# Top-k attention with a tanh-shrink layer: the first matrix of the last two units as seven products of quarters

## The chip, the core and the metric

The kernel runs on one core of one Trainium2 chip. A core has five engines with queues of their own that meet through semaphores: TensorE (PE, matrix products; PEld are its weight loads), VectorE (DVE), ScalarE (ACT), GpSimd (POOL) and SyncE (SP, which issues most transfers). The metric is the device time of one execution in microseconds, as a median over runs; less is better. The profile comes from one execution of its own, with a time of its own; its span is the stretch between the first and the last instruction that the profiler saw.

## The reference

```
scores = 1/sqrt(D) * q @ k^T                 # B=8, H=8, S=576, D=64, fp32
kth    = the 32nd largest of each row
attn   = softmax of the scores >= kth, 0 elsewhere, sum + 1e-9
x      = attn @ v, heads side by side: 4608 tokens x 512
h      = x @ w_in                            # 512 x 2048
g      = h - tanh(h)
out    = g @ w_out                           # 2048 x 512
```

All of it is fp32. The change concerns `h = x @ w_in` and `g` for the last 512 of the 4608 tokens.

## The kernel before

**Steps.** `plan` lists the attention as steps: a step is 128 queries of a pair of heads (`hp`, 4 pairs) of one batch element. A step goes through `scores` (PE), `search` (DVE, the 32nd largest of each row), `threshold` (POOL), `mask` (ACT L436, then POOL L439 and L443: z and the flags `bad`), `expo` (ACT L459), the reciprocal (DVE, `invert`, L478), `divide` (ACT L485), `turn_z` (DVE transposition of blocks, L517), `spread_keys` (SP: out to DRAM and back, L522 and L534) and five steps later `values` (PE L582, then the copy ACT L602 into the activations `xT` or `xTr`). The function `between(i)` puts the reciprocal, `divide` and `turn_z` of the step before last into the search of the current step; after the last step (n == NS) no search is left, and they follow each other.

**Units.** When the four pairs of heads of a token block are there, it becomes a unit of the feed-forward part: 17 units of 256 tokens (tag xT; xTr for the remainders, 64 rows of each of four batch elements) and two of 128. The last two of all are the unit of the remainders of b 4 to 7 (here "rest", complete in the first half of b 7) and the unit of the query tiles 2 and 3 of b 7 ("last"). A unit of 256 is 30 items of work:

- 16 items of `ffn_h`: 8 matmuls each (two column halves by `by_columns`, w_in stationary, 256 tokens moving), and after every second item tanh and copy on ACT out of a PSUM bank (L652, L653) and a subtract on POOL (L654) into `g`, which has two buffers of 128x2048.
- 14 items of `ffn_p`: the second matrix as seven products of quarters (the `ORDER` of Strassen and Winograd), each in two halves k, in two PSUM banks hx and hy that take turns. The sums of quarters of g (`sum_up`, L727) and the joins of the result (L774) are done by POOL, the copies out of PSUM by ACT (L786 to L803). The sums of w_out's quarters were made once, earlier, by POOL (`combine`), and lie in `more` and in DRAM.

**Order.** The order on each engine is the order in which the program issues (`manual_schedule`). Per step, `rate` works out how many items are to be dealt, from the work at hand and the units that come, and `deal` puts them between the parts of the step. What is left after the last step is issued at the end, `for x in work`. Buffers that come from a pool (`thpool` 4, `gpool` 2, `kqpool`, `scpool`, `tpool`, `ldpool`) wait for the last reader of the buffer that they take over.

**The end.** After the last step: a reduction of all flags `bad` on DVE (L1086), a product of one column, and a branch to an exact second run, which isn't taken with these inputs.

Of the kernel before, what the change touches and what calls it, by code (L numbers as in the profile page):

```python
# [8 lines left out]
AF = mybir.ActivationFunctionType  # L9
ALU = mybir.AluOpType  # L10
FP32 = mybir.dt.float32
# [8 lines left out]
J = 4  # L20
# [20 lines left out]
class Unit:  # L41
# [3 lines left out]
    def __init__(self, blocks, tag):  # L45
        self.blocks, self.tag = blocks, tag
        self.n = 128 * len(blocks)
        self.combines = False
        self.items = 16 if self.n == 128 else 30
        self.xT = None  # L50
        self.g = []
# [3 lines left out]
def kernel(  # L55
# [9 lines left out]
    nc = tc.nc  # L65
    P = nc.NUM_PARTITIONS
    B, H, S, D = q.shape
# [44 lines left out]
    def h_bank(k, name):  # L112
        return h_ps.tile([P, 512], FP32, tag=f"h{k}", name=name)

    def next_h(name):
        bank[0] ^= 1
        return h_bank(bank[0], name)
# [243 lines left out]
    def search(n, exact, between):  # L361

        x = st[n]
        sc, ps = x["sc"], x.pop("ps")
        m = x["m"] = mpool.tile([P, 2, TOP], FP32, tag="m", name="m")
        rounds = TOP // 8  # L370
        if exact:
            whole = ab[:, 0 : 2 * S].rearrange("p (t k) -> p t k", t=2)
            seen = [[sc[:, t].rearrange("p s k -> p (s k)") for t in range(2)]]
            seen += [[whole[:, t] for t in range(2)]] * (rounds - 1)
            left = seen[1:]
        else:
            top = x["top"] = tpool.tile([P, 2, S4 + Q], FP32, tag="top", name="top")
            near, far = ps[:, :, 0, 0:S2], sc[:, :, 1, :]
            a, b = half_max, ps[:, :, 0, S2 : S2 + S4]
            nc.vector.tensor_tensor(b, near[:, :, S4:], far[:, :, S4:], ALU.max)  # L380
            nc.vector.tensor_tensor(a, near[:, :, 0:S4], far[:, :, 0:S4], ALU.max)  # L381

            def thirds(y):
                return y.rearrange("p t (r k) -> p t r k", r=NL)

            nc.vector.tensor_tensor(low[:, :, :, 0:W2], thirds(near), thirds(far), ALU.min)  # L386
            nc.vector.tensor_tensor(low[:, :, ::-1, W2:], thirds(a), thirds(b), ALU.min)
            nc.vector.tensor_tensor(top[:, :, 0:S4], a, b, ALU.max)  # L388
            for t in range(2):
                for i in range(NL):  # L390
                    o = S4 + 8 * i
                    nc.vector.max(top[:, t, o : o + 8], low[:, t, i, :])  # L392
            seen = [[top[:, t, 0:S4] for t in range(2)], [top[:, t] for t in range(2)]]
            seen += [[rest[:, t] for t in range(2)]] * (rounds - 2)
            left = [seen[0], *seen[2:]]
        between(-1)
        for i in range(rounds):
            m8 = slice(8 * i, 8 * i + 8)
            for t in range(2):
                nc.vector.max(m[:, t, m8], seen[i][t])  # L400
            if i < rounds - 1:
                for t in range(2):
                    nc.vector.match_replace(left[i][t], m[:, t, m8], seen[i][t], NEG)  # L403
            between(i)
# [210 lines left out]
    def xt(u):  # L615
        if u.xT is None:
            p = xpool if u.tag == "xT" else xrpool
            u.xT = p.tile([P, CD, N], FP32, tag=u.tag, name=u.tag)
        return u.xT
# [3 lines left out]
    def by_columns(acc, lhs, rhs, start, stop):  # L623

        for t in range(2):
            nc.tensor.matmul(  # L626
                acc[half(t)], lhs[:, half(t)], rhs, start=start, stop=stop, skip_group_check=True
            )
# [83 lines left out]
    def quarters(u, k):  # L712

        x = u.g[k][:].rearrange("p m (f t n) -> p m f t n", f=2, t=2)
        return [[x[:, :, f, t, :] for f in range(2)] for t in range(2)]

    def sum_up(u, k, x, ms=slice(0, 4)):

        (a11, a12), (a21, a22) = quarters(u, k)
        s1 = sums[k]  # L720
        out_, a, b, op = {
            "S1": (s1, a21, a22, ALU.add),
            "S3": (a21, a21, a11, ALU.subtract),
            "S2": (a11, s1, a11, ALU.subtract),
            "S4": (a12, a12, a11, ALU.subtract),
        }[x]
        nc.gpsimd.tensor_tensor(out_[:, ms], a[:, ms], b[:, ms], op)  # L727

    ORDER = [("A11", "B11"), ("A12", "B21"), ("S2", "T2"), ("S3", "T3"), ("S1", "T1"), ("A22", "T4"), ("S4", "B22")]
    def bring(x):  # L730
# [103 lines left out]
    def ffn(u):  # L834

        nh = CF * u.n // (2 * P)
        full = len(u.blocks) == 2
        for item in range(nh):
            f = (item + 1) * CF // nh - 1
            yield CD * (f // FJ + 1), u, lambda item=item: (ffn_full if full else ffn_h)(u, item)  # L840
        if not full:
            for part in range(CF // 2):
                yield CD * (WJ + part // 2 + 1), None, lambda part=part: ffn_small_o(u, part)
            return
        for item in range(2 * len(ORDER)):
            yield 2 * WJ * CD, None, lambda item=item: ffn_p(u, item)
# [5 lines left out]
    def plan():  # L852
        steps.clear(), done.clear()

        def block(b, qt):
            return [(slice(0, P), out[b * S + qt * P : b * S + (qt + 1) * P, :])]

        rest = None
        for b in range(B):
            if b % 4 == 0:  # L860
                rest = Unit(
                    [
                        [(half(i), out[(b + k + i) * S + JP : (b + k + i + 1) * S, :]) for i in range(2)]
                        for k in (0, 2)
                    ],
                    "xTr",
                )

            parts = [(0, 1), (2, 3)]
            if b == 0:  # L870
                parts[0:1] = [(0,), (1,)]
            for a, qts in enumerate(parts):
                unit = Unit([block(b, qt) for qt in qts], "xT")
                pe = b == 0
                unit.combines = pe and a == 1
                for hp in range(NHP):
                    for i, qt in enumerate(qts):
                        steps.append(Step(b, hp, qt, unit, 0, i, len(qts), pe, a))
                    if hp == NHP - 1:
                        done[len(steps) - 1] = unit  # L880
                    if hp % 2 and a == (0 if b == B - 1 else len(parts) - 1):
                        steps.append(Step(b, hp - 1, J, rest, b % 4 * R, pe=pe, part=a))
                        if hp == NHP - 1 and b % 4 == 3:
                            done[len(steps) - 1] = rest
        for g, after in zip(steps, steps[1:]):
            if after.pe and not after.rem and not g.pe:
                g.lag = 3
# [4 lines left out]
    def run(exact):  # L892
# [80 lines left out]
        def here(i):  # L973
            return 0 <= n + i < NS
# [55 lines left out]
        for n in range(-4, NS + LAG):  # L1030
            pe = here(-2) and steps[n - 2].pe
            def due():
                for m in (n - LAG, n - LAG + 1, n - LAG + 2):
                    if 0 <= m < NS and steps[m].last and steps[m].lag == n - m:
                        values(m)

            if n < NEAR:
                due()
            share, usable, now[0] = rate(), converted[0], n
            if pe:  # L1040
                w = turn_pe(n - 2)
                next(w)
            if here(-1):
                mask(n - 1, exact)
            if here(0):
                search(n, exact, between)
            elif here(-2):
                for i in (-1, 0, LATE):
                    between(i)
            if pe:  # L1050
                spread(n - 2)
            deal(0.0 if pe else 0.4)
            if n >= NEAR:
                due()
            for x in coming_back:
                next(x, None)
            coming_back.clear()
            if here(1):
                scores(n + 1)
            if pe:  # L1060
                next(w)
            if here(0):
                threshold(n, exact)
            if here(-1):
                expo(n - 1)
            deal(0.8 if pe else 0.2)
            if pe and steps[n - 2].last:
                values(n - 2)
            deal(0.0 if pe else 0.2)
            if here(-2) and not pe and steps[n - 2].last:  # L1070
                coming_back.append(spread_keys(n - 2))
                next(coming_back[0])
            for fn in todo.pop(n, []):
                fn()
            deal(0.2)
# [48 lines left out]
```

## Time and profile before

| what | us |
|---|---|
| median of 3 runs (1480.71, 1480.95, 1483.43) | 1480.95 |
| profiled execution, its own time | 1481.03 |
| its span | 1479.2 |
| PE busy | 1371.2 (93%) |
| DVE busy | 1281.5 (87%) |
| POOL busy | 1113.0 (75%) |
| ACT busy | 1030.9 (70%) |
| mean granted clock of PE | 0.974 |

Shares over the whole span mix two stages. Up to about 1310 us every step's search runs on DVE; after that DVE's share falls to nothing in the slices of the profile and PE's is 9 tenths or more. The changed units lie in that last stage. An instruction's record gives its start and duration; on PE, neighbouring records overlap, so the start-to-start distance is what a matmul costs. A fp32 matmul of this kernel leaves two records.

### The profile page before, as it was taken

The page shows a single profiled execution, that of the slowest core. Times are in us where ns is not written, and L with a number is a line of the kernel's source. Part 1 is how long each engine was busy: PE and PEld are TensorE (multiplying, and loading weights), DVE is VectorE, ACT ScalarE, POOL GpSimd, SP SyncE. Part 2 cuts the span into 40 slices and gives each one's busy share as a digit, 9 for nine tenths or more (in the row PEclk, how much of TensorE's full clock was granted, in tenths as well). Part 3 has the DMA queues.
Part 4 walks back from the last instruction along what each step waited for, and adds up shares of the span by engine and source line. Part 5 has one row for each costly group of instructions (what it writes and reads, how often), then busy time and mean ns, then how long its engine had stood idle before and what let it go on. Part 6 is the DMA issues. An engine that isn't in the chain of part 4 may idle for free.

```text
span 1479.2 us, 35177 instructions
## 1 busy us (share of the span) xinstructions
PE 1371.2 (93%) x12036; PEld 876.7 (59%) x12036; DVE 1281.5 (87%) x4906; ACT 1030.9 (70%) x1922; POOL 1113.0 (75%) x1607
## 2 busy tenths in 40 slices
PE   4667898889999898999999999999999999999998
PEld 2455565556666565656666666666665666656665
DVE  7999887999999999999999999999999999873000
ACT  4776677768787777777777777777777777664221
POOL 3887689968788786969696969696878797766523
PEclk9788999999999999999999999999999999999999
DMA  9955102776776676676766766667666666633311
GB/s 263 360 219 184 28 21 70 192 197 161 193 182 187 162 195 178 170 194 161 179 182 185 170 181 168 175 162 203 172 180 180 166 165 189 174 106 118 101 30 46
DMA packets 241084, 242.25 MB, mean 164 GB/s; under 512 B 177408, under 2 KB 185600, under 8 KB 233728
## 3 DMA queue, kind: packets, MB, share of 16 engines
q1 hardware_dynamic: 239120, 239.69, 60.0%
q8 instruction: 98, 1.61, 0.5%
q14 instruction: 90, 0.74, 0.2%
q10 hardware_dynamic: 1776, 0.22, 0.1%
HBM read 153.99 MB, written 85.85 MB: 162 GB/s over the span
## 4 chain that ended last, share of the span: by engine, by line
PE 44%; DVE 35%; POOL 9%; DMA 5%; ACT 4%; issue 2%; SPq 1%; DVEq 0%; ACTq 0%; POOLq 0%
PE hps L626 17%; PE hx L626 8%; PE hy L626 6%; DVE m L400 6%; PE scps L350 5%; PE av L582 5%; DVE top L392 5%; DVE zx L517 4%; DVE rest L403 4%; DVE ab L386 3%; POOL z L439 3%; DVE top L403 2%; DVE ab L381 2%; POOL g L654 2%; DVE scps L380 2%
## 5 line engine op out<-in xcount | busy, mean ns | idle before, releaser
L439 POOL TENSOR_TENSOR z<-sc,z 128x576 f32<-128x576 f32 x288 | 407.5, 1437 | 66.7 <-ACT z L436 66.3
L626 PE MATMUL hps<-xT,w_in 128*64 128x256 f32 x3840 | 435.8, 382 | 3.5 <-ACT g L653 3.5
L626 PEld LDWEIGHTS hps<-xT,w_in 128*64 128x64 f32 x3840 | 270.0, 137 | 160.0 <-issue 24.0
L654 POOL TENSOR_TENSOR g<-g,th 128x512 f32<-128x512 f32 x144 | 184.5, 1282 | 93.6 <-ACT g L653 91.8
L485 ACT ACTIVATE z<-z,rd 128x576 f32<-128x576 f32 x252 | 181.1, 767 | 83.9 <-DVE rd L478 82.1
L459 ACT ACTIVATE z<-z,nb 128x576 f32<-128x576 f32 x288 | 222.0, 777 | 13.0 <-POOL z L439 12.9
L436 ACT ACTIVATE z<-sc,tb 128x576 f32<-128x576 f32 x288 | 208.4, 776 | 25.1 <-POOL tb L417 20.0
L358 ACT COPY sc<-scps 128x1152 f32<-128x1152 f32 x144 | 161.1, 1118 | 49.9 <-PE scps L350 49.4
L392 DVE MAX8 top<-ab 128x8 f32<-128x144 f32 x864 | 194.7, 295 | 0.0
L517 DVE STREAM_TRANSPOSE zx<-z 128x1152 f32<-128x1152 f32 x126 | 171.6, 1362 | 23.7 <-ACT z L485 18.0
L350 PE MATMUL scps<-kT,qT 64*128 64x288 f32 (+1 forms) x1120 | 160.8, 438 | 30.1 <-DVE top L388 29.0
L400 DVE MAX8 m<-rest 128x8 f32<-128x168 f32 x576 | 161.6, 322 | 0.0
L400 DVE MAX8 m<-top 128x8 f32<-128x144 f32 (+1 forms) x576 | 152.8, 307 | 0.0
L350 PEld LDWEIGHTS scps<-kT,qT 64*128 64x128 f32 (+1 forms) x1120 | 87.8, 180 | 88.8 <-ACT z L436 26.4
L652 ACT ACTIVATE th<-hps 128x512 f32<-128x512 f32 x144 | 84.7, 588 | 71.9 <-PE hps L626 65.7
L626 PE MATMUL hx<-w_out,g 128*64 128x256 f32 x1088 | 129.6, 385 | 2.5 <-POOL g L654 2.5
L626 PE MATMUL hy<-more,g 128*64 128x256 f32 x1088 | 125.4, 380 | 0.0
L417 POOL TENSOR_SCALAR tb<-m 128x1 f32<-128x1 f32 x288 | 84.6, 303 | 31.7 <-DVE m L400 31.3
L386 DVE TENSOR_TENSOR ab<-scps,sc 128x576 f32<-128x576 f32 x144 | 107.7, 748 | 0.0
L626 PEld LDWEIGHTS hx<-w_out,g 128*64 128x64 f32 x1088 | 76.4, 138 | 49.5 <-POOL g L654 5.8
L626 PEld LDWEIGHTS hy<-more,g 128*64 128x64 f32 x1088 | 76.7, 137 | 42.9 <-issue 6.0
L443 POOL TENSOR_SCALAR bad<-top,tb 128x3 uint8<-128x3 f32 x288 | 97.1, 344 | 0.1
(126 smaller groups left out, 2349.6 us busy)
## 6 DMA issues: line engine op xcount, KB each, us to landing
there<-zx SPq DMA_DIRECT2D x56, 1152.0 KB, 4.8
spare<-there SPq DMA_DIRECT2D x224, 288.0 KB, 5.5
more<-kept_T SPq DMA_DIRECT2D x34, 512.0 KB, 3.8
out_dram<-ot SPq DMA_DIRECT2D x32, 256.0 KB, 2.9
there<-zx SPq DMA_DIRECT2D x14, 576.0 KB, 6.8
spare<-there SPq DMA_DIRECT2D x56, 144.0 KB, 3.1
vb<-in_v_dram SPq DMA_DIRECT2D x48, 128.0 KB, 5.4
kin<-in_k_dram SPq DMA_DIRECT2D x84, 72.0 KB, 4.4
```

What stands on the lines that cost most here:

```text
L350: nc.tensor.matmul(ps[rows, t, s, 0:S2], qT[g.b, g.hp + i, g.part][half(t), qs], kT[g.b, g.hp + i][half(t), ks], start=True, stop=True,)
L358: nc.scalar.copy(sc[:], ps[:, :, :, 0:S2])
L386: nc.vector.tensor_tensor(low[:, :, :, 0:W2], thirds(near), thirds(far), ALU.min)
L392: nc.vector.max(top[:, t, o : o + 8], low[:, t, i, :])
L400: nc.vector.max(m[:, t, m8], seen[i][t])
L436: nc.scalar.activation(zv[:, t, :], scf[:, t, :], AF.Relu, bias=tb[:, t : t + 1], scale=-BIG)
L439: nc.gpsimd.tensor_tensor(zv[:, t, :], scf[:, t, :], zv[:, t, :], ALU.subtract)
L459: nc.scalar.activation(x["zv"][:, t, :], x["zv"][:, t, :], AF.Exp, bias=x["nb"][:, t : t + 1], scale=scale, accum_out=den[:, t : t + 1],)
L485: nc.scalar.activation(x, x, AF.Copy, scale=rds[n][:, g.i, t : t + 1])
L517: nc.vector.transpose(tiles(zx, g.nq)[:, :, :, g.i, :].rearrange("p c k j -> p k c j"), z[:].rearrange("p (k c j) -> p k c j", c=NG, j=G),)
L626: nc.tensor.matmul(acc[half(t)], lhs[:, half(t)], rhs, start=start, stop=stop, skip_group_check=True)
L654: nc.gpsimd.tensor_tensor(g, g, th[:], ALU.subtract)
```

## The change

`Unit.tail` marks the last two units. For them the first matrix is done by 14 items of `ffn_s` in place of 16 of `ffn_h`, so such a unit has 28 items. `ffn_s` runs the same seven products as `ffn_p`, twice (k = 0, 1: the first and the second 1024 columns of w_in), each of 16 matmuls with 64 stationary columns and 128 moving tokens. The quarters are halves of the 512 rows and of the columns for w_in, halves of the rows and of the 256 tokens for x.

- `sides(k)` forms S1 to S4 of w_in[2k] and w_in[2k+1]: 8 instructions of 128x512 on DVE. `sides(0)` stands after the reciprocal and `divide` of step NS−2, `sides(1)` after its `turn_z`. The 16 results go to places that the attention no longer uses (`places`: ab, et_rem, one buffer of kin, four of kT, one of vb, three of sc).
- `tokens(u)` forms T1 to T4 of the unit's activations: 4 instructions of 128x256 on DVE, at the unit's first item.
- A product is copied out of PSUM by ACT; `join` adds on DVE, tanh on ACT, the subtract on POOL.
- `sum_up` of a tail unit (sums of quarters of g for the second matrix) runs on DVE; on POOL in all other units.

In the order of the instructions: on PE the scores of the last step and the values of head pair 1 of the last batch stand earlier against the first-matrix work around them; on ACT the masks of the last two steps (L436) stand one copy earlier. SP's order is the same.

```diff
@@ -46,6 +46,7 @@
         self.blocks, self.tag = blocks, tag
         self.n = 128 * len(blocks)
         self.combines = False
+        self.tail = False
         self.items = 16 if self.n == 128 else 30
         self.xT = None
         self.g = []
@@ -714,6 +715,106 @@
         x = u.g[k][:].rearrange("p m (f t n) -> p m f t n", f=2, t=2)
         return [[x[:, :, f, t, :] for f in range(2)] for t in range(2)]
 
+    left, right_of = {}, {}
+
+    def places():
+
+        yield from (ab[:, 0:512], ab[:, 512:1024], et_rem[:, 0:512], et_rem[:, 512:1024])
+        yield ldpool.tile([P, S], FP32, tag="kin", name="kin")[:, 0:512]
+        for x in range(NHP):
+            yield kqpool.tile([P, S], FP32, tag="kT", name="kT")[:, 0:512]
+        y = kqpool.tile([P, 2, J, D], FP32, tag="vb", name="vb", bufs=3)[:]
+        yield y.rearrange("p t c d -> p (t c d)")
+        for x in range(3):
+            y = scpool.tile([P, 2, 2, S2], FP32, tag="sc", name="sc")[:].rearrange("p t s k -> p (t s k)")
+            yield from (y[:, 0:512], y[:, 512:1024])
+
+    def sides(k):
+
+        for j in (2 * k, 2 * k + 1):
+            w = w_in[j][:].rearrange("p (q c) (m r n) -> p q c m r n", q=2, m=2, r=2)
+            (a11, a12), (a21, a22) = [[w[:, q, :, :, r, :] for q in range(2)] for r in range(2)]
+            new = []
+            for x in range(4):
+                new.append(next(space[0]).rearrange("p (c m n) -> p c m n", c=2, m=2))
+            s1, s2, s3, s4 = new
+            nc.vector.tensor_tensor(s1, a21, a22, ALU.add)
+            nc.vector.tensor_tensor(s2, s1, a11, ALU.subtract)
+            nc.vector.tensor_tensor(s3, a11, a21, ALU.subtract)
+            nc.vector.tensor_tensor(s4, a12, s2, ALU.subtract)
+            left[j] = {"A11": a11, "A12": a12, "A22": a22, "S1": s1, "S2": s2, "S3": s3, "S4": s4}
+
+    space = [None]
+
+    def tokens(u):
+
+        x = xt(u)[:].rearrange("p (q c) (t n) -> p q c t n", q=2, t=2)
+        (b11, b12), (b21, b22) = [[x[:, q, :, t, :] for t in range(2)] for q in range(2)]
+        ys = [rest[:].rearrange("p t k -> p (t k)")]
+        for i in range(2):
+            ys.append(tpool.tile([P, 2, S4 + Q], FP32, tag="top", name="top")[:].rearrange("p t k -> p (t k)"))
+        ys.append(ldpool.tile([P, S - 2 * P], FP32, tag="qin", name="qin")[:])
+        t1, t2, t3, t4 = [y[:, 0 : 2 * P].rearrange("p (c n) -> p c n", c=2) for y in ys]
+        nc.vector.tensor_tensor(t1, b12, b11, ALU.subtract)
+        nc.vector.tensor_tensor(t2, b22, t1, ALU.subtract)
+        nc.vector.tensor_tensor(t3, b22, b12, ALU.subtract)
+        nc.vector.tensor_tensor(t4, b21, t2, ALU.subtract)
+        right_of[u] = {"B11": b11, "B21": b21, "B22": b22, "T1": t1, "T2": t2, "T3": t3, "T4": t4}
+
+    def ffn_s(u, item):
+
+        k, i = item // len(ORDER), item % len(ORDER)
+        if item == 0:
+            tokens(u)
+        if i == 0:
+            cur[u] = [next_h("hx"), None]
+            u.g.append(gpool.tile([P, 4, 512], FP32, tag="g", name="g"))
+        if i == 1:
+            cur[u][1] = h_bank(bank[0] ^ 1, "hy")
+        acc = cur[u][i % 2][:].rearrange("p (m n) -> p m n", n=P)
+        a, b = ORDER[i]
+        for m in range(4):
+            lhs = left[2 * k + m // 2][a][:, :, m % 2, :]
+            for c in range(2):
+                by_columns(acc[:, m, :], lhs[:, c, :], right_of[u][b][:, c, :], i in (0, 1, 3) and m + c == 0, m == 3 and c == 1)
+        (g11, g21), (g12, g22) = quarters(u, k)
+
+        def own(x):
+            return thpool.tile([P, 512], FP32, tag="th", name=x)[:].rearrange("p (m n) -> p m n", n=P)
+
+        def join(x, y):
+            nc.vector.tensor_tensor(x, x, y, ALU.add)
+
+        def shrink(x, y):
+            th = own("th")
+            nc.scalar.activation(th, y, AF.Tanh)
+            if y is not x:
+                nc.scalar.copy(x, y)
+            nc.gpsimd.tensor_tensor(x, x, th, ALU.subtract)
+
+        if i in (0, 3, 5):
+            y = own("hp")
+            nc.scalar.copy(y, acc)
+            if i == 5:
+                join(g21, y)
+                shrink(g21, g21)
+            else:
+                u.part = y
+        elif i == 1:
+            nc.scalar.copy(g11, acc)
+            join(g11, u.part)
+            shrink(g11, g11)
+        elif i == 2:
+            nc.scalar.copy(g21, acc)
+        elif i == 4:
+            nc.scalar.copy(g22, acc)
+            join(g22, u.part)
+            shrink(g22, g22)
+        else:
+            shrink(g12, acc)
+            for x in ("S1", "S3"):
+                sum_up(u, k, x, slice(0, 2) if k else slice(0, 4))
+
     def sum_up(u, k, x, ms=slice(0, 4)):
 
         (a11, a12), (a21, a22) = quarters(u, k)
@@ -724,7 +825,8 @@
             "S2": (a11, s1, a11, ALU.subtract),
             "S4": (a12, a12, a11, ALU.subtract),
         }[x]
-        nc.gpsimd.tensor_tensor(out_[:, ms], a[:, ms], b[:, ms], op)
+        engine = nc.vector if u.tail else nc.gpsimd
+        engine.tensor_tensor(out_[:, ms], a[:, ms], b[:, ms], op)
 
     ORDER = [("A11", "B11"), ("A12", "B21"), ("S2", "T2"), ("S3", "T3"), ("S1", "T1"), ("A22", "T4"), ("S4", "B22")]
     def bring(x):
@@ -835,6 +937,10 @@
 
         nh = CF * u.n // (2 * P)
         full = len(u.blocks) == 2
+        if u.tail:
+            nh = 0
+            for item in range(2 * len(ORDER)):
+                yield CD * WJ, u, lambda item=item: ffn_s(u, item)
         for item in range(nh):
             f = (item + 1) * CF // nh - 1
             yield CD * (f // FJ + 1), u, lambda item=item: (ffn_full if full else ffn_h)(u, item)
@@ -871,6 +977,10 @@
                 parts[0:1] = [(0,), (1,)]
             for a, qts in enumerate(parts):
                 unit = Unit([block(b, qt) for qt in qts], "xT")
+                unit.tail = b == B - 1 and a == len(parts) - 1
+                if unit.tail:
+                    rest.tail = True
+                    unit.items = rest.items = 4 * len(ORDER)
                 pe = b == 0
                 unit.combines = pe and a == 1
                 for hp in range(NHP):
@@ -1044,6 +1154,13 @@
                 mask(n - 1, exact)
             if here(0):
                 search(n, exact, between)
+            elif n == NS:
+                space[0] = places()
+                between(-1)
+                between(0)
+                sides(0)
+                between(LATE)
+                sides(1)
             elif here(-2):
                 for i in (-1, 0, LATE):
                     between(i)
```

## The prediction

> **What bounds the kernel now.** I read the chain of waits first, because the change touches only the last two units of 256 tokens: "rest" (the remainders of b 4 to 7, activations xTr) and "last" (b 7, query tiles 2 and 3, xT). Columns: start us, us, what.
>
> ```profile
> 1340.52 0.65 PE hx L626 x4
> 1341.17 3.45 PE hy L626 x32
> ...
> 1358.44 3.45 PE hx L626 x32
> 1361.89 1.73 PE hps L626 x16
> 1363.62 2.16 PE av L582 x20
> 1365.78 25.90 PE hps L626 x240
> 1391.68 1.73 PE hx L626 x16
> ...
> 1418.01 2.16 PE av L582 x20
> 1420.17 27.63 PE hps L626 x256
> 1447.79 3.45 PE hx L626 x32
> ...
> 1468.51 3.48 PE hx L626 x32
> 1471.99 0.02 issue
> 1472.01 0.37 ACT ot L803
> ```
>
> From 1340.5 to 1472.0 the chain is TensorE alone. The first matrix of a unit costs 27.63 us there (rest: 1.73 + 25.90), and what follows it starts at once. The end after 1472 (copy, output transfer, closing wait: 7.2 us) is not touched. The table of stretches confirms it (length, then busy PE, PEld, DVE, ACT, POOL, then clock, DMA share and GB/s):
>
> ```profile
> 1362.00:1418.00 56.00, 56.00 (x522) 37.29 (x520) 3.88 (x4) 14.63 (x31) 24.12 (x25) 1.00 0.33 91
> 1420.00:1448.00 28.00, 28.00 (x262) 18.68 (x260) 0.00 (x0) 7.99 (x16) 12.81 (x11) 1.00 0.03 7
> ```
>
> PE is full at full clock and DVE is empty. So PE work removed here is time removed, and a new wait of PE is time added. The other engines matter only through what arrives too late. For that I read each engine's timeline around the last score steps (start, us, engine, ...; idle before in brackets):
>
> ```profile
> 1347.80 1.38 DVE L517 STREAM_TRANSPOSE zx<-z 128x1152 f32<-128x1152 f32 x1 [3.86 <-ACT z L485]
> 1352.25 0.17 DVE L478 RECIPROCAL rd<-rd 128x2 f32<-128x2 f32 x1 [3.07 <-POOL rd L469]
> 1363.22 1.05 DVE L1086 TENSOR_REDUCE anybad<-bad 128x1 f32<-128x864 uint8 x1 [10.81 <-POOL bad L443]
> 1364.19 1.37 DVE L517 STREAM_TRANSPOSE zx<-z 128x1152 f32<-128x1152 f32 x1
> ...
> 1376.90 1.38 DVE L517 STREAM_TRANSPOSE zx<-z 128x1152 f32<-128x1152 f32 x1 [8.67 <-ACT z L485]
> ```
>
> DVE has no work but these; the reduction over `bad` sits 10.8 us idle behind POOL and everything behind it on DVE waits too.
>
> **What the Trainium skill says.** "VectorE: DVE Perf Modes", its Trainium2 errata, prices an fp32 add of two tensors at (N+151)/0.96 ns: 691 at 512, 424 at 256 elements. The trace agrees where nothing disturbs: 673 ns median in the first row below. "SBUF — State Buffer", "Who interferes with whom": a DVE instruction with two SBUF inputs and a GpSimd one that reads SBUF exclude each other for the whole instruction. The third row is what that looks like (min/median/max ns; the same instruction with POOL at work):
>
> ```profile
> L202 DVE SCALAR_TENSOR_TENSOR f<-w_out,e x10: 664/673/682, 17.8 to 78.4; 128x512 uint32<-128x512 uint32 x10
> ...
> L202 DVE SCALAR_TENSOR_TENSOR f<-spare,f x8: 678/1376/1562, 91.2 to 150.7; 128x512 uint32<-128x512 uint32 x8
> ```
>
> "TensorE: Matmul & The Clock Gate", Part 1: the clock is granted by a window of recent activity, so an idle PE can cost twice. The trace has one case: 2.33 us idle at 1311.1 were followed by half clock for 3.4 us (mean clock 0.57 over 1314 to 1318), about 1.7 us lost; three other gaps of 2.6 to 3.1 us were not.
>
> **The change, part by part** (all against the profiled execution, span 1479.2, its own time 1481.03, which is the median of the runs, 1480.95, within 0.1).
>
> *1. Fewer multiplications.* Each fp32 matmul leaves two records here (the code issues 128 matmuls for the 256 of a unit), so I count in pairs of records. Per unit 128 pairs of 64x256 become 14 products of 16 pairs of 64x128. Today's 128 pairs take 27.63, 0.216 a pair. The narrower form is shown by
>
> ```profile
> 102.40 1.09 PE L582 MATMUL av<-et,vb 128*64 128x128 f32 x14
> ```
>
> seven pairs, where the starts after the first pair are 0.109 us apart: half of 0.216. A product is 16 × 0.109 = 1.747, a unit 24.46, the gain 3.17; two units −6.35. The bounds: 0.108 (exactly half, −6.9 for both) below, above 0.125 (the row with its slow first: 1.09 less one matmul's 0.27 is 0.82, over 6.5 pairs).
>
> *2. The order around it.* The two units have 28 work items (14 and 14) where they had 30 (16 and 14), so the shares dealt out per step shift by one. On PE the last step's scores move ahead of half of a 24-matmul block of the preceding full unit (scores and last search some 1.7 us earlier), and the 1.73 us that rest now begins with, before the values of head pair 1, goes behind them. That unit's first product then no longer meets POOL's subtract at 1339.19, for which PE stands now between matmuls that start at 1340.19 and 1340.52. The seven products of that unit end some 0.45 earlier and the values at 1363.46. Bounds 0 and −0.6. On ACT the masks of the last two steps (L436, 1.44 us a pair) stand one copy earlier in the queue; for the last step that copy is the one at 1358.54, so POOL's last z pair (now 1359.76, behind it) can go some 3.5 us earlier, ahead of POOL's join for that copy, which has 0.73 us and no hurry. SP's order does not change.
>
> *3. The 16 sums of w_in on DVE.* sides(0), 8 adds, goes after the reciprocal, 1351.2 to 1355.6 by 0.60 a start (1358.4 where POOL's z blocks two of them; the places they are written to are free since the last search and scores ended at 1344). Nothing waits for it but `bad`: its z pair grows from 2.79 to about 3.3, as earlier pairs under two-input DVE work did (3.23 to 3.44). `bad` ends at 1360.4. Then on DVE: the reduction 1.05, turn 1.38, sides(1) 8 adds from 1362.7 at 0.60 plus 0.05 for each dependent one (5.1), T1 and T2 0.9: T2 is there at 1368.7. PE does two products after the values (A11, A12) and wants S2·T2 at 1363.46 + 3.49 = 1366.95. **PE waits 1.8.** Without the exclusion 1.1. With sides(1) after the tokens it would be nothing, but that isn't the order.
>
> *4. Joins and copies of rest's first half.* Per half: 7 PSUM copies or tanh on ACT (0.58, start to start 0.49), 3 joins and two sums on DVE (0.69), tanh from SBUF (taken as 0.72, between the PSUM 0.60 at 512 and the SBUF 0.76 at 576), 4 POOL subtracts (1.28). The products take turns in two PSUM banks, so product i+2 waits for the copy of i; at 1.75 us a product that has a microsecond of slack. It fails once: the second half's first two products go to the banks whose copies (item 5, and the quarter g12 of item 6) stand on ACT behind the last step's normalising pair (1.43, waiting for DVE's reciprocal), and behind a tanh which waits for a DVE join queued behind the last 1.38 us turn. With item 6 ending at 1377.5, item 5's copy ends at 1377.95 (**wait 0.5**); turn until 1378.9, join 1379.5, tanh 1380.3, tanh and copy of g12 until 1381.25, so the next product starts at 1381.3 instead of 1379.75 (**wait 1.55**). Bounds: 0 (if that pair runs before, in a gap), and 3.5 (if POOL's subtracts also block the join).
>
> *5. Last unit.* No score work is left, so only the exclusion bites: the join of g21 meets POOL's subtract of g22 and is 1.2 us late, **0.7**; 0 without it. Its four token sums (1.4) are done before item 2, 3.5 us after the start.
>
> *6. Nothing.* The sums of the second matrix move from POOL to DVE (0.69 for 1.28): the earliest is needed two products, 3.5 us × 2, after its inputs. Buffers for the joins (th) turn over every 3 products, later than any reader. SP's transfers for the last step feed values that PE reaches at 1395 and 1418.
>
> Sum: −6.35 − 0.45 + 1.8 + 2.05 + 0.7 = **−2.25**: span 1476.95, time 1481.03 − 2.25 = 1478.8, and below the median of the runs by as much: **1478.7**.
>
> **Rivals.**
> - *The waits are smaller* (DVE and POOL exclude each other seldom, ACT takes the copies sooner): only the 1.1 and 2.05 remain, −3.65, 1477.3; with no wait at all −6.8, 1474.2. For it: DVE is idle 10 us in the stretch, and the exclusion needs both at once. Against: the reduction's place behind `bad` is fixed.
> - *The waits cost clock.* Each of the two waits at 1367 and 1379 may be followed by 3.4 us at half clock: +1.7 once, 1480.4; twice 1482.1. For: the case at 1314. Against: three gaps longer than mine did nothing, mine are under 2 us.
> - *Slower: the narrow stream.* If 64x128 pairs, where weight loads (137 ns in the rows, against matmuls half as long as before) come twice as often in a microsecond, run at 0.125 instead of 0.109, the 448 pairs of both units cost 7.2 more: 1485.9. It decides from 0.121 a pair on (then +5.3, past 1483.9). For: the 0.82/6.5 above. Against: 64x64 pairs run at 0.058 in the values of the remainders, so loads can follow.
>
> **Chances.** Forecast (waits of 3.5 to 5.5) 0.42; smaller waits 0.30; clock or longer waits, still at or under before's 0.2% 0.15; slower 0.13. A difference of 0.2% (3 us: 1478.0 and 1483.9) is what a measurement of this kernel can tell from none; my forecast lies just inside it. Of the first case a third lies below 1478.0: faster 0.30 + 0.14 = 0.44; same 0.28 + 0.15 = 0.43; slower 0.13. Range: 1474.4 (hardly a wait) to 1482.6 (twice clock and a little). The forecast alone: 1477.4 to 1479.9.
>
> **What would show it.** PE's matmul group of hx and hy with 128x128 in two stretches of 24.5 us plus gaps; an idle gap of 1 to 2 us before the third product of rest, released by DVE's T2; another before the ninth, released by ACT's g; DVE adds of 0.69, some at 1.2 to 2 during POOL's z; clock 1.00 from 1362 on. Wrong: pairs well over 0.109, a clock under 0.9 after 1366, gaps in the second matrix, or no gaps at all.

## The result, and the profile after

| | before | after |
|---|---|---|
| median of 11 runs each, us | 1483.43 (1480.23 to 1484.9) | 1480.26 (1478.54 to 1480.92) |
| ratio after / before | | 0.9983, 95% interval 0.9975 to 0.9991 |
| profiled execution, its own time | 1481.03 | 1480.84 |
| its span | 1479.2 | 1479.0 |

The ratio stands for −2.5 us (−3.7 to −1.3); the two medians lie 3.2 apart; forecast were −2.25. The absolute time is 1.6 above the forecast of 1478.7: the kernel before itself came out 2.5 higher over these runs than in the three that were shown ahead.

The two spans differ by 0.2 only, which has to be taken apart first. In every trace TensorE stands idle for 2.3 us once, shortly before the scores of the last step but one. The time from the end of that gap to the end of the last product is called the *stretch* here; its work is the same in both kernels up to the two units. The chain of waits in this stretch begins as follows in the kernel before, first in the trace shown ahead, then in a second trace of the same kernel (`before_again`):

```profile
1313.41 2.66 PE hps L626 x16
1316.08 2.09 PE scps L350 x8
```

```profile
1317.38 1.95 PE hps L626 x16
1319.33 1.17 PE scps L350 x8
```

The first ran 3.4 us at half clock behind the gap and lost 1.64 (0.71 and 0.92 in the two lines, before rounding) that the second didn't lose. The stretch is 158.55 in the first and 156.92 in the second, 154.78 in the changed kernel, which had full clock there too. So the change took **2.14 us** at equal clock. That the spans show only 0.2 has to do with where the gap fell: it ended at 1313.41 in the first trace and at 1317.30 in that of the changed kernel, 3.9 later, for reasons that lie before 1310. This nearly cancels the 3.8 by which the stretch is shorter there (2.1 from the change, 1.6 from the clock). An unedited second trace of the kernel before has its gap at 1317.38, so the shift isn't the change's.

The new chain of waits, around the first matrix of rest (start us, us, what):

```profile
1363.75 1.37 DVE zx L518
1365.12 0.58 DVE kT L741
...
1369.56 0.60 DVE sc L744
1371.10 1.97 PE hx L627 x32
1373.07 1.75 PE hy L627 x32
...
1378.48 1.43 ACT z L486 x2
1380.43 1.99 PE hx L627 x32
1382.52 0.58 ACT th L790
1383.10 0.48 ACT g L792
1383.62 1.97 PE hy L627 x32
1385.59 1.75 PE hx L627 x32
```

A product costs 1.75 where nothing holds it, and the chain that was TensorE alone is now broken by VectorE and ScalarE. TensorE's own timeline names the four waits (idle before it and its releaser in brackets):

```profile
1367.50 1.92 PE L627 MATMUL hy<-xTr,w_in 128*64 128x128 f32 x32
1371.10 1.09 PE L627 MATMUL hx<-top,ab 128*64 128x128 f32 x16 [1.68 <-DVE top L759]
...
1380.43 1.97 PE L627 MATMUL hx<-xTr,w_in 128*64 128x128 f32 x32 [0.37 <-ACT hp L797]
1383.62 1.97 PE L627 MATMUL hy<-xTr,w_in 128*64 128x128 f32 x32 [1.23 <-ACT g L792]
...
1437.21 1.97 PE L627 MATMUL hy<-xT,w_in 128*64 128x128 f32 x32 [0.42 <-ACT g L792]
```

A record ends some 0.2 us after the next one could begin, so the loss is read from starts: the third product was due at 1367.50 + 1.75 = 1369.25 and began at 1371.10, 1.85 late; in the same way 0.57, 1.44 and, in the last unit, 0.59. What stands ahead of T2 (L759) on VectorE is the order that was foreseen:

```profile
1358.95 1.90 DVE L744 TENSOR_TENSOR kT<-w_in,kT 128x512 f32<-128x512 f32 x1
1362.78 1.05 DVE L1203 TENSOR_REDUCE anybad<-bad 128x1 f32<-128x864 uint8 x1 [1.94 <-POOL bad L444]
1363.75 1.37 DVE L518 STREAM_TRANSPOSE zx<-z 128x1152 f32<-128x1152 f32 x1
1365.05 0.65 DVE L741 TENSOR_TENSOR kT<-w_in 128x512 f32<-128x512 f32 x1
...
1370.53 0.42 DVE L759 TENSOR_TENSOR top<-xTr,rest 128x256 f32<-128x256 f32 x1
```

The clock stayed at 1.00 through all of it, here from 1366 to 1394 (length, then busy PE, PEld, DVE, ACT, POOL, then clock, DMA share and GB/s), and also in the windows from there to 1473:

```profile
1366.00:1394.00 28.00, 24.72 (x446) 24.02 (x444) 12.14 (x21) 13.78 (x26) 7.67 (x7) 1.00 0.31 86
```

### The profile page after: what moved, and what is told of

It reads as the page before. It is cut to its first block, busy times and chain, and to the rows that moved or that the text cites. A ratio compares the mean times of both kernels' runs of the same rounds, so it can differ in the third digit from the quotient of the medians.

```text
span 1479.0 us, 35995 instructions
## 1 busy us (share of the span) xinstructions
PE 1369.1 (93%) x12420; PEld 891.0 (60%) x12420; DVE 1318.2 (89%) x4962; ACT 1038.6 (70%) x1934; POOL 1091.9 (74%) x1587
## 4 chain that ended last, share of the span: by engine, by line
PE 49%; DVE 30%; POOL 7%; DMA 6%; ACT 3%; issue 2%; SPq 1%; DVEq 0%; ACTq 0%; POOLq 0%
PE hps L627 16%; PE hx L627 10%; PE hy L627 8%; PE scps L351 6%; PE av L583 6%; DVE m L401 5%; DVE zx L518 4%; DVE top L393 4%; DVE rest L404 4%; DVE ab L387 2%; POOL z L440 2%; DVE top L404 2%; DMA vb<-in_v_dram 2%; DVE ab L382 2%; PE hps L641 1%
## 5 line engine op out<-in xcount | busy, mean ns | idle before, releaser
L627 PE MATMUL hps<-xT,w_in 128*64 128x256 f32 x3584 | 410.8, 384 | 3.5 <-ACT g L654 3.5
L627 PEld LDWEIGHTS hps<-xT,w_in 128*64 128x64 f32 x3584 | 252.7, 138 | 153.3 <-issue 26.8
L655 POOL TENSOR_TENSOR g<-g,th 128x512 f32<-128x512 f32 x128 | 163.9, 1281 | 63.8 <-ACT g L654 62.3
L653 ACT ACTIVATE th<-hps 128x512 f32<-128x512 f32 x128 | 75.0, 586 | 40.0 <-PE hps L627 36.4
L381 DVE TENSOR_TENSOR scps<-scps,sc 128x288 f32<-128x288 f32 x144 | 64.0, 444 | 36.9 <-ACT sc L359 36.9
```

Source lines behind the costliest of these rows:

```text
L627: nc.tensor.matmul(acc[half(t)], lhs[:, half(t)], rhs, start=start, stop=stop, skip_group_check=True)
L655: nc.gpsimd.tensor_tensor(g, g, th[:], ALU.subtract)
```

## The experiments

Stretches are compared, since a run's time also holds the 6 us by which the stretch's start wanders. Each stretch comes from one trace, and each trace has a time axis of its own.

**The kernel before again.** No edit.

> The kernel before once more, for its clock. If the half clock of 3.4 us that follows the 2.3 us gap near 1312 in its profile (1.6 us lost) is a matter of where the gap falls, it may be missing here, and the stretch from the gap's end to the last product is 156.9 instead of 158.6. If it belongs to this kernel's order, it is there again at the same place.

Measured: full clock behind the gap, stretch 156.92. The half clock isn't part of this kernel's order.

**The wait for T2.** Four runs. The first puts the token sums ahead of sides(1):

```diff
             tokens(u)
+            for x in later_sides[:3]:
+                x()
+            del later_sides[:3]
...
             join(g11, u.part)
+            while later_sides:
+                later_sides.pop(0)()
...
-                sides(1)
+                sides(1, add_later)
```

`add_later` only stores the eight sums in `later_sides`; they are issued at the two places above.

> The token sums of rest are put ahead of the 8 sums of sides(1) on VectorE, and these fill its idle time behind them (3 after the tokens, 5 after the first join). Theory (the wait of 1.68 us before the third product of rest is the queue on VectorE: reduction, turn, 8 adds, T1, T2): T2 is there by 1367.5 on the changed kernel's time axis, the third product follows the second at once, the later waits (0.4 idle before the eighth, 1.2 before the ninth, 0.4 in the last unit) stay as they are, and the time falls by 1.7 to 1.9 us against the changed kernel. Rival (T2 only comes last; the activations or the weights' sums are as late): the gap stays over 1 us, released by another tile. Second rival (the wait moves): the adds make the joins late and the gap comes back at the fourth to sixth product.

Measured: stretch 152.88 (−1.90), time 1478.46, ratio to before 0.9974 (0.9964 to 0.9984). The gap ahead of the third product is gone, those of 0.38, 1.23 and 0.42 stayed. The queue theory holds; neither rival does. What in the queue was at fault, the next ones ask. The reduction was written behind the block of the hand-made order, and was nevertheless placed ahead of the turn; written inside that block it comes behind all sums, at 1456.2:

```diff
         run(False)
+        any_bad = xpool.tile([P, 1], FP32, tag="anybad", name="anybad")
+        nc.vector.reduce_max(any_bad[:], ...)
-    any_bad = xpool.tile([P, 1], FP32, tag="anybad", name="anybad")
-    nc.vector.reduce_max(any_bad[:], ...)
```

The second theory below arose because the sum into the buffer vb began at 1365.73 in the changed kernel, just as the values ended at 1365.76.

> The changed kernel with the reduction over the flags issued as the last instruction of VectorE instead of ahead of the last but one turn. Queue theory (T2 is late because the turn and sides(1) stand behind the reduction, which waits for GpSimd): everything behind it comes 1.9 us earlier, the gap before the third product (1.68 us) goes. Two-locks theory (the second sum of sides(1) goes to the buffer of values vb, which TensorE reads until the values end at 1365.76 on the changed kernel's axis; it started at 1365.73 there): the first sum of sides(1) starts near 1362, the second still not before 1365.7, and the gap stays between 1.5 and 1.8 us.

Measured: stretch 152.88 and no gap ahead of the third product. The near coincidence at 1365.7 was chance. Here the values end at 1368.04 on this trace's axis (the start of rest's first product), and the sum into vb began 3.0 us before that, with the turn directly behind sides(0):

```profile
1363.08 1.36 DVE L518 STREAM_TRANSPOSE zx<-z 128x1152 f32<-128x1152 f32 x1
1364.37 0.64 DVE L741 TENSOR_TENSOR kT<-w_in 128x512 f32<-128x512 f32 x1
1365.05 0.69 DVE L742 TENSOR_TENSOR vb<-kT,w_in 128x512 f32<-128x512 f32 x1
...
1370.38 0.42 DVE L759 TENSOR_TENSOR top<-xTr,rest 128x256 f32<-128x256 f32 x1
```

So this sum didn't wait for these values. The two companions agree:

> The changed kernel with the buffer vb given out as the last of the 16 places, so that the second sum of sides(1) goes to a score buffer. Two-locks theory: the reduction still ends near 1363.8 and the turn near 1365.1, the sums follow as before, the gap before the third product stays between 1.6 and 1.8. Rival (the buffer alone holds sides(1)): the gap falls by over 0.5.

Measured: gap 1.67, stretch 154.76. As the changed kernel; moving the buffer does nothing.

> Both of the two edits. Two-locks theory: the turn starts about 1360.9 on the changed kernel's axis, the 8 sums follow it to 1367.3, T2 is there at 1368.2, before the third product is due (1369.25): its gap goes, and the stretch from the end of the 2.3 us gap to the last product falls from 154.8 to 152.7 to 153.0. If a third lock exists, the gap stays over 0.5 and its releaser names it.

Measured: stretch 152.88, the same as with the flags alone. Moving the reduction, which nothing needs before the end, was enough by itself: in the changed kernel it brought 1.94 us of idle VectorE and 1.05 of its own. It wasn't the only thing in the way: T2 was 1.85 late, and the run with the tokens first removed the same wait by taking the eight sums (5.0 us) from ahead of it. Either edit alone is enough.

**The waits between the halves.**

```diff
-            if i == 5:
-                join(g21, y)
-                shrink(g21, g21)
-            else:
-                u.part = y
+            u.part = y
...
             shrink(g12, acc)
+            join(g21, u.part)
+            shrink(g21, g21)
```

> The tanh and copy of g12 (seventh product) are issued ahead of the join and tanh of g21 on ScalarE. Theory (the ninth product waits for the copy of g12, which stands behind a tanh that waits for a join on VectorE, itself behind the last turn in rest and behind GpSimd's subtract in the last unit): both waits before the second half's second product go, 1.2 us idle in rest and 0.4 in the last unit (1.4 and 0.6 in the chain), the 0.4 before the eighth stays, the time falls by 1.9 to 2.0 against the changed kernel. Rival (the bank itself or ScalarE's load of copies is the limit): the gap shrinks by less than half, since the same copies are to be done. Second rival: g21 comes later and its sums make a new wait of 1 us or more later in the second half.

Measured: stretch 152.77 (−2.01), time 1478.11, ratio to before 0.997 (0.9957 to 0.9983). What went are the 1.44 in rest and the 0.59 in the last unit, 2.03 together. Of the gaps only the 1.70 ahead of the third product and the 0.37 ahead of the eighth are left. ScalarE's timeline of this run shows why, and why the 0.37 stays:

```profile
1380.41 1.43 ACT L486 ACTIVATE z<-z,rd 128x576 f32<-128x576 f32 x2
1381.74 0.56 ACT L797 COPY hp<-hy 128x512 f32<-128x512 f32 x1
1382.20 0.60 ACT L790 ACTIVATE th<-hx 128x512 f32<-128x512 f32 x1
1382.69 0.58 ACT L792 COPY g<-hx 128x512 f32<-128x512 f32 x1
1383.85 0.63 ACT L790 ACTIVATE th<-g 128x512 f32<-128x512 f32 x1 [0.58 <-DVE g L786]
```

The bank of g12 is now free before the tanh that waits for VectorE. The copy of the sixth product (hp) still stands behind the normalising pair.

**The order around the last step**, without any of the new arithmetic:

```diff
+        groups = [(item,) for item in range(nh)]
+        if u.items == 28:
+            groups = [(0, 1)] + groups[2:8] + [(8, 9)] + groups[10:]
```

> The kernel before with the same arithmetic, the 16 first-matrix items of the two units dealt as 14, which gives the order on TensorE that the changed kernel has around the last step (scores 8 matmuls earlier, the values of head pair 1 before rest's first item). Theory (that order is worth 0.54 us, since the second matrix of the preceding unit no longer meets GpSimd's subtract): the 0.16 gap of TensorE near 1340 is gone and the stretch is 156.3 to 156.5, against 156.95 in the kernel before at full clock (1.6 more if the half clock falls behind the 2.3 us gap). Rival (the 0.54 belongs to the items of 1.75 us): stretch 156.8 to 157.0.

Measured: the gap of 0.16 is gone, and the preceding unit's first product is whole. Two lines of the kernel before (`before_again`), then that product in this run:

```profile
1339.50 3.19 PE L626 MATMUL hx<-w_out,g 128*64 128x256 f32 x28
1342.86 0.65 PE L626 MATMUL hx<-w_out,g 128*64 128x256 f32 x4 [0.16 <-POOL g L654]
```

```profile
1341.67 3.62 PE L626 MATMUL hx<-w_out,g 128*64 128x256 f32 x32
```

From its start to that of the next product it took 3.84 us there and 3.46 here. The half clock fell behind the 2.3 us gap (first 24 matmul records 4.76 us instead of 3.12); stretch 158.18, less 1.64 is 156.54, or −0.38 against 156.92. The order is worth 0.38, not the expected 0.54; the rival's 156.8 isn't reached.

**The sums of quarters of g on GpSimd**, as in all other units:

```diff
-        engine = nc.vector if u.tail else nc.gpsimd
+        engine = nc.gpsimd
```

> The changed kernel with the sums of quarters of g for the two units back on GpSimd. Theory (moving them to VectorE was needed for nothing but room): per unit S1, S3 of both halves, S2 and S4, some 9 us of GpSimd work, fit beside its four subtracts of 1.28 per half; the gaps stay within 0.1 of those of the changed kernel and the stretch is 154.6 to 155.0; the 0.4 gap of the last unit stays or shrinks, as VectorE has no sums in front of its joins. Rival (GpSimd's queue takes the subtracts of the second half late): a gap of 0.5 to 2.5 us in the first three products of the second matrix, stretch over 155.3.

Measured: stretch 155.79, +1.01. The expectation missed: the rival's gap is there, in the last unit's second matrix, while the four gaps of the first matrices are as they were:

```profile
1455.92 1.95 PE L627 MATMUL hx<-more,g 128*64 128x256 f32 x16 [0.46 <-POOL g L829]
1457.96 1.95 PE L627 MATMUL hx<-et,g 128*64 128x256 f32 x16
```

Due at 1455.29 and 1457.65, so 0.63 and another 0.31 late. Moving these sums to VectorE is a needed part of the change, worth about 1 us by this one trace.

**All waits removed.** Four runs led there (e3_all_three, e9_waits_removed, e10_no_waits, e12_no_waits_late_keys). All issue g12 first and defer the last step's reciprocal, normalising pair, turn and transfers; the first two put the tokens first, the other two the reduction last:

```diff
-            elif here(-2):
-                for i in (-1, 0, LATE):
-                    between(i)
+            elif n == NS + 1:
+                last_step.extend([... invert, divide, turn_z, spread_keys ...])
```

> Both of the above, and the last step's reciprocal, normalising pair, turn and transfers are issued after the fourteenth product of rest, the sums S1 and S3 of the first half after the first join of the second. Theory: no idle time of TensorE over 0.1 us from the first product of rest to the last of the last unit; both first matrices take 24.45 us; the stretch from the end of the 2.3 us gap near 1315 to the last product is 4.3 to 4.5 us shorter than in the changed kernel (154.8), so 150.3 to 150.5, and the time falls by as much against it, 6 to 7 against the kernel before. Rival (VectorE and ScalarE have too little room for the work at 1.75 us a product): new gaps that sum to over 1.5 us. Second rival (the last step's transfers become the end of a wait): a gap before the values at the start of the last unit.

Measured: 1492.76 us, ratio 1.0067. The gaps of the first matrix are gone, but TensorE stood 16.09 us before the values of head pair 2. In this run and in e10_no_waits the transfers were issued before those values, whose weights they overwrite, so both computed head pair 2 with head pair 3's weights; their times count for the waits alone. It is the second rival, in a harsher form than I had thought of.

> As the run of all three, but the second half of the last step's transfers is issued after the values of the pair before, whose weights lie in the same buffer (in that run they were overwritten first, so it computed other values for head pair 2, and TensorE waited 16 us for these transfers). Theory: no gap of TensorE over 0.1 us between the first product of rest and the last product; the stretch from the end of the 2.3 us gap to the last product is 150.0 to 150.5 (after: 154.8; the two repairs alone: 152.9 and 152.8); the time is 4 to 5 us below the changed kernel and 6 to 7 below the kernel before. Rival (the deferred work of the last step makes a wait of its own, in the second half's copies or before the values of the last pair): gaps of 0.5 us or more there, stretch over 151.

Measured: stretch 151.78, time 1478.88, ratio 0.9949 (0.9935 to 0.9963; the kernel before had a median of 1484.79 there). One gap is left, of the rival's kind but on a queue that I hadn't named: SyncE's. The transfers of the last step, issued after the fourteenth product, are late, and a transfer into `more` stands behind them on SyncE's queue. (It brings the T2 of the second matrix, a sum of w_out's quarters, not the token sum of the first matrix.)

```profile
1412.12 1.90 PE L627 MATMUL hy<-more,g 128*64 128x256 f32 x16
1415.39 1.95 PE L627 MATMUL hy<-more,g 128*64 128x256 f32 x16 [1.37 <-DMA more<-kept_T]
```

> The changed kernel with the reduction over the flags last on VectorE, g12 ahead of g21 on ScalarE, the sums S1 and S3 of the first half behind the next half's first join, and the last step's reciprocal, normalising pair, turn and transfers after the seventh product of rest instead of around the fifth (the run with the waits removed had them after the fourteenth, and SyncE's queue was late by that: a transfer of T2's sums into more held TensorE for 1.4 us). Theory: no gap over 0.1 us after the one of 2.3 us near 1316; the stretch from its end to the last product is 150.2 to 150.5 (154.8 in the changed kernel, 156.9 to 158.6 before); time 6 to 7 us below the kernel before, 4.4 below the changed one. Rival (the normalising pair, wherever it stands, costs the copies behind it a wait): a gap of 0.3 to 1.5 in the first three products of the second half. Second rival (SyncE is late still): the gap before the third product of the second matrix stays.

Measured: half clock behind the 2.3 us gap; stretch 153.02, 151.38 without its 1.64, so outside what was expected; gaps of 0.07 ahead of the tenth product and of 0.68 before the values of head pair 2, on the transfers that were too early. Time 1477.82, ratio 0.9963.

> As the run named e10_no_waits, but the second half of the last step's transfers is issued after the values of the pair before, as in the changed kernel (in e10_no_waits they overwrote the weights of head pair 2 first, so that run computed other values there and TensorE waited 0.68 us for them at these values). Theory: the gap of 0.68 before the values goes, the 0.07 before the eighth product may stay; the stretch from the end of the 2.3 us gap to the last product is 150.3 to 150.7 at full clock, 1.6 more if the half clock falls behind that gap; time 4 us below the changed kernel, 6 to 7 below the kernel before. Rival: SyncE's queue is late by the later turn and T2's transfer makes a gap near the third product of the second matrix (1.4 us in e9_waits_removed), stretch over 151.5.

Measured: stretch 152.00 with the half clock (the first 16 records 3.47 instead of 1.95, so 1.52), 150.48 without it; one gap of 0.07, ahead of the tenth product. Time 1476.06 (6 runs), ratio to before 0.9954 (0.9938 to 0.9970). Without the half clock the stretch is the shortest of all; by the ratio this version can't be told from e9_waits_removed (0.9949). Its interval lies below that of the changed kernel (0.9975 to 0.9991), and it holds nothing but the changed kernel's arithmetic in another order. In the last unit its chain is TensorE alone again:

```profile
1429.05 3.49 PE hx L627 x64
1432.55 1.75 PE hy L627 x32
...
1441.28 5.20 PE hx L627 x64
1446.48 3.45 PE hy L627 x32
...
1463.75 3.48 PE hx L627 x32
```

## Why the prediction was right

| step | forecast | measured | from |
|---|---|---|---|
| 1. products instead of the plain matrix, two units | −6.35 | −6.33 | 2 × 14 × 1.747 = 48.92 for 55.25 |
| 2. order around it | −0.45 | −0.38 | TensorE's work ahead of rest's own: 48.46 for 48.84; −0.38 also with the order alone |
| 3. wait for T2 | +1.8 | +1.85 | start of the third product; −1.90 when taken away |
| 4. waits between rest's halves | +2.05 | +2.01 | 0.57 and 1.44 |
| 5. last unit | +0.7 | +0.59 | start of its ninth product |
| first matmuls after a wait, slower | – | +0.12 | 0.02 to 0.05 each after four waits, by what the two first matrices (28.39 and 25.10) hold beyond products and waits |
| sum | −2.25 | −2.14 | stretch 154.78 against 156.92 |

Point by point:

- *The bound.* TensorE was full, so every term carried through to the end. No term is off by more than 0.12. That the sum is within 0.11 is in part luck: the last unit came out 0.11 shorter, and the slower first matmuls after a wait, 0.12 together, which the prediction left out, made up for it.
- *Products.* 0.109 us a pair held over 448 pairs; the slower rival, which needed 0.121, had nothing.
- *T2's wait.* Right in size and in place. That it hung on the reduction, which step 3 named, was then shown (taken away alone: −1.90). The price of the sums held: 0.69 at 512 elements and 0.42 at 256 beside an idle GpSimd (the row shown for it ahead is of another instruction with two inputs). Beside a busy one, two of the sums took 1.22 and 1.90, and the GpSimd pair that stands ahead of `bad` 3.68 instead of the estimated 3.3:

```profile
1357.36 1.12 POOL L876 TENSOR_TENSOR ot<-ot,oy 128x256 f32<-128x256 f32 x1 [3.52 <-ACT ot L899]
1358.44 3.68 POOL L440 TENSOR_TENSOR z<-sc,z 128x576 f32<-128x576 f32 x2
```

```profile
1357.81 1.22 DVE L743 TENSOR_TENSOR kT<-w_in 128x512 f32<-128x512 f32 x1
```

The sum at 1357.81 ended at 1359.03, 0.55 after GpSimd's join; the one of 1.90 ended at 1360.85, again 0.55 after the first half of the pair. So the two engines took turns, as the exclusion that the Trainium skill describes ("SBUF — State Buffer", "Who interferes with whom") has it. Its share in the wait is an estimate from these durations and those of the same instructions beside an idle VectorE: the join took 1.12 for 0.73 and the pair 3.68 for 2.79, some 1.3 us together, where the prediction gave it 0.7. A run that takes away the exclusion alone wasn't made.
- *The halves.* That step 4 has two causes was shown: issuing g12 earlier took away the 1.44 and, in the last unit, the 0.59, not the 0.57; the 0.57 went when the normalising pair was moved as well. That this run gained 2.01, just what rest's two waits sum to, is chance.
- *Last unit.* The join did meet GpSimd's subtract (1433.64 to 1434.92) and took 1.40 instead of 0.69, ending 0.55 after it; that is 0.7 longer, not 1.2. The wait of 0.59 needed the order of ScalarE's copies too: with g12 issued earlier it was gone, although the join still took 1.39.
- *Second matrix.* Step 6 priced the sums' move at nothing, and as the change has them nothing is late. Left on GpSimd they cost 1.0, which the prediction didn't say.
- *The clock.* Behind the gaps of 0.4 to 1.7 us in the stretch no half clock followed in any trace, so the rival "the waits cost clock" had no part in it. It did fall behind the gap of 2.3 us, in 4 of 14 traces; the last section shows what decided it. The prediction speaks of one such case, but its trace has a dozen stretches at half clock before the end, eleven of them before 571 us.
- *The level.* The time fell by as much as the sum says, within the interval; the level of 1478.7 was tied to three runs of the kernel before, two of which lay low.

## What to carry to other kernels

When the bound engine has no slack, saved work pays in full and each new wait is paid in full: here 6.7 us were saved and 4.6 given back, and 4.3 of these came back when nothing but the order was changed. Look for an instruction that nobody needs soon but that waits (here a reduction over flags, placed ahead of a turn and of ten sums), and for the queue order of PSUM copies, where one that needs only its bank should not stand behind one that needs another engine. When a step is deferred, follow its transfers on their queue as well: deferred once too far they held TensorE for 1.4 us, issued too early they overwrote what was still read.

## What the runs showed of the hardware that was not expected

- After one and the same gap of 2.33 us half clock followed in 4 of 14 traces, lasted 3.41 us and cost 1.5 to 1.64 us. The Trainium skill says ("TensorE: Matmul & The Clock Gate", Part 1) that the clock's window is free-running and 3413 ns long, and the traces agree: within a trace, every change of the granted clock from 50 us on lies on one grid of 3.413 us. Laid over the gap, the grid tells the cases apart. First the trace shown ahead, then `before_again`, each an interval of the grid that holds the larger part of the gap and the one after it (columns as above):

```profile
1311.08:1314.50 3.42, 1.09 (x11) 0.77 (x12) 3.42 (x20) 3.26 (x6) 2.08 (x4) 1.00 0.00 0
1314.50:1317.91 3.41, 3.41 (x16) 1.67 (x12) 1.23 (x1) 0.00 (x0) 2.23 (x5) 0.50 0.41 173
```

```profile
1313.36:1316.77 3.41, 1.70 (x16) 0.86 (x12) 3.41 (x20) 1.83 (x4) 2.71 (x4) 1.00 0.00 1
1316.77:1320.19 3.42, 2.81 (x24) 1.75 (x24) 2.94 (x10) 1.53 (x4) 2.78 (x3) 1.00 0.00 0
```

  The first gap lies wholly in one interval, which leaves TensorE 2.3 us idle there; the second is split, 1.7 and 0.6. In the four traces with half clock, the interval that holds most of the gap has 2.03 to 2.32 us of idle TensorE in it; in the ten others it has 1.32 to 1.84. The same border parts all 5375 grid intervals at full clock between 100 and 1470 us in the 14 traces, by the records of TensorE's matmuls: 132 were followed by half clock, and none of these held less than 2.01 us of idle time; of the 5243 that weren't, none held more than 2.01. In the changed kernel no interval behind the 2.3 us gap holds more than 1.7. So it was not the kernel's order that decided, but where the gap fell on the grid, and that differs from run to run.
- A comparison of two single profiles can be off by that much: here 0.2 us of span stood for a change of 2.1.
- The stretch's start wandered between 1313.4 and 1319.8 us over 14 traces, as much as the whole effect of the best version; the kernel before had medians from 1480.95 to 1484.79 in the groups of runs.
